# Retention and softplus FFN on one core: the first unit in whole chunks, with later weight loads and an exchanged pair of heads

## Chip, cores and metric

One core of a Trainium2 chip. The metric is the device time of the kernel in microseconds; before the change the median of three runs is 817.8 us (817.5 to 818.37).

## What is computed

```python
def _attn_ref(q, k, v):                       # batch 8, heads 8, sequence 576, head dim 64
    scores = 1.0 / np.sqrt(D_) * np.matmul(q, k.transpose(0, 1, 3, 2))
    gamma = 1.0 - 2.0 ** (-5.0 - np.arange(H))
    Dmat = np.where(rel >= 0, gamma[:, None, None] ** rel[None, :, :], 0.0)
    return np.matmul(scores * Dmat, v)

def _moe_ref(x, w_in, w_out):                 # 4608 tokens, 512 -> 2048 -> 512
    h = x @ w_in
    g = np.maximum(h, 0.0) + np.log1p(np.exp(-np.abs(h)))
    return g @ w_out
```

The result is `_moe_ref(_attn_ref(q, k, v))`, the heads side by side as the 512 model columns. `w_in` and `w_out` arrive as 64-bit floats.

## The kernel before

**Retention.** The 4608 tokens are 36 *chunks* of 128. A chunk is two *steps*: step 2c holds heads 0 to 3 of chunk c, step 2c+1 heads 4 to 7. A step has two pairs of heads (`s`), and a head of 64 rows fills half of the array's rows. Per step TensorE makes the *scores* (keys by queries, L195; in the opening L360), the *sums* (keys by values, from which a running state is made, L211; L375), the *values* product (masked scores by values, L299; L397) and the *cross* product (earlier state by queries, L311; L402). Around them: the values are scaled (`scale_values`, L188 on GpSimd, L191 on ScalarE), the scores masked (`scores_out` L253, `masked_whole` L367, VectorE), the state updated (`states_out`, L280 to L293; `state_whole`, VectorE and GpSimd), and the result x put in `xt` as a high and a low part (`halves_out`, `half_x`; `values_out`).

**FFN.** A *unit* is 512 tokens. In the first unit, the loop `for i in range(NF)` goes over the 16 blocks of 128 hidden columns: h(i) (`hidden_mm`, 12 matmuls of 128x512, L475), softplus of it (ScalarE: Abs L483, Exp L484, Ln L485; VectorE: `softplus` L489), its split in a high part (ScalarE, `softplus_split` L493) and a low one (VectorE, `softplus_rest` L497), together g(i), then y(i) (`output_mm`, 12 matmuls, L510 or L518), which is issued one iteration later, behind h(i+1). Each of the two PSUM banks of h serves every other i.

**Weights.** Each block has two *pieces* of 128x512, win (for h) and wout (for y). A piece is loaded (`load_weight` L564, 512 KB) in one of five buffers and turned into high and low parts by five operations, which the text calls p (ScalarE, `weight_p` L574), t (VectorE, L581), b (VectorE, L587), c (ScalarE, L599) and d (VectorE, L604). After d the buffer's next load is issued and a win is written back to DRAM (`weight_store` L608).

**The opening** does steps 0 to 7 (the first unit's tokens) before the loop, loads in a hand-written order on SP's queue, and also handles step 8's scores and sums and three weight pieces. In the loop every odd i does one attention step: scores and sums of step m, values and cross of step m-1, in a bank of their own. After the loop come ten *plain slots* p (product L892, retention of a whole chunk at every even p by `chunk_products`, y of the slot before), then the rest, whose code stays. `chunk_products` takes two steps at once in two banks, `two` (scores and results) and `third` (sums). Since two row groups of the array must not write one bank at once, a tiny memset on GpSimd (`mark`) stands between the sums of the first row group and those of the second.

Engines run their own instructions in the order written; a wait holds up all that is behind it. What sets the order is the code's own order.

```python
    first_a, first_b = {3: 0, 5: 1, 6: 2}, {4: 0, 6: 1}
    first_weights = {4: (0,), 6: (1,), 7: (2,), 8: (3,)}
```

Of the kernel before, what the change touches and what calls it, by code (L numbers as in the profile page):

```python
# [40 lines left out]
START_WEIGHTS = 3  # L41
OPENING = 3
NOPEN = AHEAD + 2
# [3 lines left out]
NPIECE = 2 * NF  # L47
NJ = NF // 2
OPEN1 = 6
# [20 lines left out]
LAST = 320  # L70

# [13 lines left out]
def retention_softplus_ffn(ctx: ExitStack, tc, first, whole, others, consts, w, out):  # L85
# [6 lines left out]
    const, att, moe = pool("const", 1), pool("att", 2), pool("moe", 2)  # L92
    rawp, xpool, wpool = pool("rawp", 2), pool("xpool", 1), pool("wpool", 1)
# [8 lines left out]
    later = {}  # L102
# [47 lines left out]
    def load_rest(m):  # L150
        place = later["odd"] if m >= 2 * CHUNKS - 1 and m % 2 else rawp
# [7 lines left out]
    def load_step(m):  # L159
# [8 lines left out]
        else:  # L168
            if m < NOPEN:
                place = openp if m < OPEN1 else openp2  # L170
                r = place.tile([P, 8 * C if m < FIRST else RAW], F32, name=f"raw{m}")
# [9 lines left out]
    def scale_values(m):  # L181
# [5 lines left out]
        if m >= AHEAD:  # L187
            nc.gpsimd.tensor_mul(v, v, f.unsqueeze(2).broadcast_to([P, 4, D]))  # L188
            return
# [16 lines left out]
    def sums_mm(m, s, t, h):  # L206
# [3 lines left out]
        if follows if t else start != HC:  # L210
            mm = nc.tensor.matmul(L["T"][rows[h], t, part[s]], L["kp"][rows[t], s, rows[h]], L["v"][rows[t], s, rows[h]],  # L211
                                  start=True, stop=True, skip_group_check=True)
            L.setdefault(("sums", t), []).append(mm)
# [83 lines left out]
    def values_mm(m, s, t, h, clear):  # L297
        L = live[m]
        nc.tensor.matmul(L["O"][rows[h], t, part[s]], L["v"][rows[t], s, rows[h]], L["a"][rows[t], h, s],  # L299
                         start=clear, stop=L["states"][t] is None, skip_group_check=True)  # L300

    def cross_mm(m, s, t, h):
# [4 lines left out]
        if t == h:  # L307
# [16 lines left out]
    def chunk_products(steps, done):  # L324
# [18 lines left out]
        for n in range(max(len(x) for x in pairs)):  # L343
            if n == 2 * len(steps) and sums_of(steps, 0):
                mark = nc.gpsimd.memset(later["mark"].tile([1, 1], F32, tag="mark", name="mark"), 0.0)
# [25 lines left out]
    def sums_whole(m, bank):  # L371
        L = live[m]
        for s in range(2):
            for h in range(2):
                nc.tensor.matmul(bank[rows[h], 0, TCOLS][:, part[s]], L["kp"][:, s, rows[h]], L["v"][:, s, rows[h]],  # L375
# [16 lines left out]
    def values_whole(m, bank):  # L392
        L = live[m]
        before = states.get(m % 2)
        for s in range(2):
            for h in range(2):
                nc.tensor.matmul(bank[rows[h], s, VCOLS], L["v"][:, s, rows[h]], L["a"][:, h, s], start=True,  # L397
                                 stop=before is None, skip_group_check=True)
# [81 lines left out]
    def logs(h):  # L480

        ab = moe.tile([P, T], F32, tag="ab", name="ab", bufs=ABUFS)
        nc.scalar.activation(ab, h, AF.Abs)  # L483
        nc.scalar.activation(ab, ab, AF.Exp, scale=-1.0)  # L484
        nc.scalar.activation(ab, ab, AF.Ln, bias=1.0)  # L485
        return ab

# [73 lines left out]
    def load_weight(n):  # L561
        if n < NPIECE:
            wl[n] = wst.tile([P, PIECE, 2], I32, tag="wst", name="wst", bufs=WBUFS)
            nc.sync.dma_start(wl[n].rearrange("p c a -> p (c a)"), w[n // 2, n % 2])  # L564
# [24 lines left out]
    def weight_dst(n):  # L589
        p = n // 2  # L590
        if n % 2:
# [14 lines left out]
    def weight_store(n):  # L606
        if n < NPIECE and n % 2 == 0:
            nc.sync.dma_start(split[n // 2].bitcast(F32), wins[n // 2].bitcast(F32))  # L608
# [88 lines left out]
    first_a, first_b = {3: 0, 5: 1, 6: 2}, {4: 0, 6: 1}  # L697
    first_weights = {4: (0,), 6: (1,), 7: (2,), 8: (3,)}
    fill = moe.tile([P, T], F32, tag="ab", name="fill", bufs=ABUFS)
    nc.vector.memset(fill, 1.0)  # L700
    for m in range(AHEAD):
        load_step(m)
        for n in first_weights.get(m, ()):
            load_weight(n)
    load_step(AHEAD)
    nc.sync.dma_start(consts_sb, consts)
# [13 lines left out]
    def next_scores(m):  # L720
        new = ps_open.tile([P, 2, T], F32, tag="pair", name="pair")
        if m < FIRST:
            scores_whole(m, new)
        else:
            scores(m, new)
        return new
# [4 lines left out]
    for m in range(AHEAD):  # L731
        if m < FIRST:
            bank = (ps_att if m % 2 else ps_val).tile([P, 2, T], F32, tag="bank" if m % 2 else "val", name="bank")
            sums_whole(m, bank)
            values_whole(m, bank)
            if m == 0:
                next_scores(1)
            if m + 2 < AHEAD:
                new = next_scores(m + 2)
            ready = live[m]  # L740
            if m < FIRST - 1:
                state_whole(m, ready)
            if m == 0:
                scale_values(1)
            if m + 2 < AHEAD:
                scale_values(m + 2)
            parts_out = values_out(m, nc.gpsimd if m < FIRST - 1 else nc.vector)
            if m == 0:
                masked_whole(1)
            if m + 2 < FIRST:  # L750
                masked_whole(m + 2)
            if m == FIRST - 1:
                weight_b(2)
            parts_out()
            if m == FIRST - 1:
                weight_c(2)
            if m == FIRST - 1:
                scale_values(AHEAD)
                state_whole(m, ready)
        else:  # L760
            sums(m, new)
            scores_out(m)
            states_out(m)
        if m in first_a:
            weight_a(first_a[m])
        if m in first_b:
            weight_b(first_b[m])
            weight_c(first_b[m])
        if m == 5:
            weight_dl(0)  # L770
        if m == AHEAD - 1:
            weight_d(2)
        if m == AHEAD - 2:
            load_step(AHEAD + 1)
    weight_dl(1)
    load_weight(WBUFS + 2)
    weight_store(2)
# [5 lines left out]
    constant[0] = constants(consts_sb[:, 0:SMALL], consts_sb[:, SMALL:])  # L783


    for i in range(NF):
        n = START_WEIGHTS + 2 * i
        m = AHEAD + (i - 1) // 2
        step = i % 2
        if step:  # L790
            bank = ps_att.tile([P, 2, T], F32, tag="bank", name="bank")
            scores(m, bank)
            sums(m, bank)
            values(m - 1, bank)
            if i < NF - 1 and m + 1 >= NOPEN:
                load_step(m + 1)
        weight_p(n)
        weight_t(n)
        weight_c(n - 1)
        if i == 1:  # L800
            weight_dl(n - 1)
        weight_b(n)
        if i:
            weight_t(n + 1)
        h = hidden_mm(i, i % 2)
        ab = logs(h)
        if i > 1:
            weight_dl(n - 1)
        if i < NF - 1:
            softplus(h, ab)  # L810
        if i == 0:
            weight_t(n + 1)
        if step:
            _, t, cols = place(m - 1)
            where = (B11, B21)[(m - 1) % 2], STAGE[(m - 1) % 2, t], cols
            halves_out(m - 1)
            scores_out(m)
            states_out(m)
            if i < NF - 1:
                scale_values(m + 1)  # L820
            if m == NOPEN:
                open_pools.close()
                place_weights(ctx.enter_context(tc.tile_pool(name="wpool2", bufs=1)), NF)
        if i == NF - 1:
            softplus(h, ab)
        weight_c(n)
        if not step:
            weight_dl(n)
        gs[0, i] = softplus_split(ab)
        softplus_rest(gs[0, i], ab)  # L830
        if step:
            weight_dl(n)
            half_x(*where, nc.gpsimd)
        weight_p(n + 1)
        weight_b(n + 1)
        if n + 2 >= NPIECE and "ring" not in later:
            weight_pools.close()
            for name, bufs in (("ring", RING), ("odd", 2)):
                later[name] = ctx.enter_context(tc.tile_pool(name=name + "2", bufs=bufs))
            load_step(2 * CHUNKS - 1)  # L840
            scale_values(2 * CHUNKS - 1)
# [8 lines left out]
    for name, bufs in (("quad", QUADS), ("mark", 2), ("sum", 1)):  # L850
        later[name] = ctx.enter_context(tc.tile_pool(name=name + "2", bufs=bufs, side="right"))
    two = later["two"] = ps_att.tile([P, 2, T], F32, tag="bank", name="two")
# [4 lines left out]
    groups = [([m + 1], [m])]  # L857
    for ch in range(m // 2 + 1, NCHUNK + 1):
        groups.append(([2 * ch, 2 * ch + 1] if ch < NCHUNK else [], [k for k in (2 * ch - 2, 2 * ch - 1) if k > m]))
    groups = groups[::-1]  # L860

    def next_steps(steps):
        ks = [k for m in steps for k in ((m + 1, m + 2) if len(steps) == 1 else (m + 2,)) if k < NSTEP]
# [11 lines left out]

    def values_taken(steps, done):
        if steps:
            scores_out(*steps)
        if done:
            halves_out(*done)  # L880

    def group_out(steps, done):
        values_taken(steps, done)
        if steps:
            states_out(*steps)
# [12 lines left out]
    def plain_slot(u, p, xa, xb, rest, group=None, blocks=(), jobs=(), starts=()):  # L898
# [3 lines left out]
        ahead = u == 1 and p == 0  # L902
        if ahead:
            chunk_products(*group)
            coming_steps = next_steps(group[0])
# [7 lines left out]
        if ahead:  # L913
            group_out(*group)
        elif group:
# [5 lines left out]
        if group and not ahead:  # L921
# [78 lines left out]
    def store_out(j):  # L1000
# [3 lines left out]
        (0, prepare, PLAIN + 1), (0, prepare_whole, PLAIN), (0, prepare_sums, PLAIN), (1, prepare_split, PLAIN),  # L1004
# [6 lines left out]
        *[(2 * j + 1, store_plain, j) for j in range(PLAIN)])  # L1011
# [443 lines left out]
```

## Time and profile before

| what | us |
|---|---|
| median of the runs (lowest, highest) | 817.8 (817.5, 818.37) |
| span of the profiled execution, first to last instruction | 815.8 |
| TensorE busy | 808.2 |
| VectorE busy | 560.6 |
| ScalarE busy | 389.2 |
| GpSimd busy | 123.7 |

The profiled execution's own time is given as its span; the runs' median is 2.0 us above it. TensorE's granted clock is 1.000 of full speed over the span. Where TensorE is busy, time goes only if it has less to do; where it is idle, if what it waits for comes sooner.

### The profile page before, as it was taken

How to read it: one execution, taken by the hardware profiler on the slowest of the kernel's cores; microseconds unless marked ns; L12 is line 12 of the kernel's file. 1: busy time of each engine (PE TensorE's matmuls, PEld its weight loads, DVE VectorE, ACT ScalarE, POOL GpSimd, SP SyncE). 2: the span in 40 equal slices, each digit the busy share in tenths (PEclk: the TensorE clock that was granted, in tenths of full speed). 3: DMA queues.
4: the chain of work that ended last, by engine and by line, in shares of the span. 5: the costliest groups of instructions: out<-in, count | busy, mean ns of one | idle time of the engine just before them, and what ended most of it. 6: DMA issues, size and time to landing. Idle time of an engine off the chain costs nothing.

```text
span 815.8 us, 18681 instructions
## 1 busy us (share of the span) xinstructions
PE 808.2 (99%) x7322; PEld 666.2 (82%) x7322; DVE 560.6 (69%) x953; ACT 389.2 (48%) x681; POOL 123.7 (15%) x223
## 2 busy tenths in 40 slices
PE   8999999999999999999999999999999999999998
PEld 6788888888888888888888888888888888888886
DVE  5999976777666774867669974555679944335785
ACT  6888863334323244434344554324355734434553
POOL 4322321320321420112122001112100000000000
PEclk9999999999999999999999999999999999999999
DMA  9998979989899882798987777878657776666674
GB/s 359 324 318 292 313 239 389 334 312 324 264 311 359 304 315 79 239 330 271 310 286 236 220 229 244 261 235 264 215 177 217 221 246 193 196 191 194 194 221 159
DMA packets 149847, 211.75 MB, mean 260 GB/s; under 512 B 10880, under 2 KB 114816, under 8 KB 149760
## 3 DMA queue, kind: packets, MB, share of 16 engines
q1 hardware_dynamic: 149760, 210.56, 78.3%
q8 instruction: 59, 0.97, 0.5%
q14 instruction: 28, 0.23, 0.1%
HBM read 168.05 MB, written 42.47 MB: 258 GB/s over the span
## 4 chain that ended last, share of the span: by engine, by line
PE 95%; DMA 2%; DVE 2%; ACT 0%; issue 0%; SPq 0%; DVEq 0%
PE acc L892 22%; PE sum L1183 20%; PE y L518 16%; PE two L892 14%; PE h L475 5%; PE two L1183 4%; PE third L892 3%; PE third L211 2%; PE third L1183 2%; PE acc L1183 2%; PE two L195 2%; PE two L299 2%; PE two L311 1%; DMA raw<-others 1%; DMA raw<-whole 1%; DVE wst L587 0%
## 5 line engine op out<-in xcount | busy, mean ns | idle before, releaser
L892 PE MATMUL acc<-xt,ring 128*128 128x512 f32 x780 | 196.4, 389 | 0.1
L892 PEld LDWEIGHTS acc<-xt,ring 128*128 128x128 f32 x780 | 146.3, 188 | 30.9 <-issue 0.3
L1183 PE MATMUL sum<-parts,ring 128*128 128x512 f32 x708 | 170.9, 392 | 0.0
L1183 PEld LDWEIGHTS sum<-parts,ring 128*128 128x128 f32 x708 | 131.6, 188 | 27.8
L1177 DVE TENSOR_TENSOR parts<-g,parts 128x512 fp32r<-128x512 f32 x168 | 115.4, 694 | 45.0 <-ACT parts L1173 42.3
L518 PE MATMUL y<-wout,g 128*128 128x512 f32 x564 | 137.2, 392 | 0.3 <-DVE g L497 0.3
L1173 ACT CAST parts<-g 128x512 fp32r<-128x512 f32 x168 | 103.9, 622 | 67.6 <-DVE parts L1177 27.3
L518 PEld LDWEIGHTS y<-wout,g 128*128 128x128 f32 x564 | 104.8, 188 | 22.9 <-DVE g L497 0.7
L892 PE MATMUL two<-xt,ring 128*128 128x512 f32 x486 | 123.3, 389 | 0.0
L892 PEld LDWEIGHTS two<-xt,ring 128*128 128x128 f32 x486 | 91.2, 188 | 18.9
L1205 ACT ACTIVATE g<-g 128x512 f32<-128x512 f32 x72 | 45.3, 629 | 59.4 <-DVE g L1220 35.6
L188 POOL TENSOR_TENSOR qv<-qv,consts_sb 128x256 f32<-128x256 f32 x61 | 47.4, 778 | 164.7 <-DMA qv<-others 157.7
L1220 DVE TENSOR_TENSOR g<-two,g 128x512 f32<-128x512 f32 x24 | 16.6, 692 | 77.8 <-PE two L892 77.8
L1218 ACT COPY g<-acc 128x512 f32<-128x512 f32 x24 | 14.1, 588 | 77.6 <-PE acc L892 77.6
L497 DVE TENSOR_TENSOR g<-ab,g 128x512 fp32r<-128x512 f32 x42 | 32.3, 769 | 26.4 <-ACT g L493 25.7
L493 ACT CAST g<-ab 128x512 fp32r<-128x512 f32 x42 | 26.1, 621 | 46.2 <-PE y L518 41.5
L475 PE MATMUL h<-xt,win 128*128 128x512 f32 x192 | 47.4, 396 | 0.3 <-DVE win L604 0.3
L475 PEld LDWEIGHTS h<-xt,win 128*128 128x128 f32 x192 | 35.3, 188 | 8.2 <-DVE win L604 0.6
L1258 ACT ACTIVATE g<-acc 128x512 f32<-128x512 f32 x24 | 14.3, 598 | 49.3 <-PE acc L892 49.3
L211 PEld LDWEIGHTS third<-qv,keys 64*64 64x64 f32 x776 | 27.0, 134 | 8.9 <-issue 7.7
L253 DVE TENSOR_TENSOR a<-two,mask 128x512 f32<-128x512 f32 (+1 forms) x28 | 19.0, 679 | 22.2 <-PE third L211 15.2
L1183 PE MATMUL two<-parts,ring 128*128 128x512 f32 x144 | 33.6, 389 | 0.0
(177 smaller groups left out, 1190.4 us busy)
## 6 DMA issues: line engine op xcount, KB each, us to landing
ring<-split SPq DMA_DIRECT2D x121, 256.0 KB, 4.9
ring<-combined SPq DMA_DIRECT2D x108, 256.0 KB, 3.9
ring<-outcombined SPq DMA_DIRECT2D x96, 256.0 KB, 3.5
qv<-others SPq DMA_DIRECT2D x61, 320.0 KB, 5.5
ring<-outsplit SPq DMA_DIRECT2D x72, 256.0 KB, 3.8
wst<-w SPq DMA_DIRECT2D x32, 512.0 KB, 5.8
keys<-others SPq DMA_DIRECT2D x61, 256.0 KB, 5.4
split<-win SPq DMA_DIRECT2D x16, 512.0 KB, 6.7
```

What stands on the lines that cost most here:

```text
L188: nc.gpsimd.tensor_mul(v, v, f.unsqueeze(2).broadcast_to([P, 4, D]))
L211: mm = nc.tensor.matmul(L["T"][rows[h], t, part[s]], L["kp"][rows[t], s, rows[h]], L["v"][rows[t], s, rows[h]], start=True, stop=True, ski ...
L253: nc.vector.tensor_mul(a[:, :, at], src.rearrange("p h (s c) -> p h s c", c=HC), mask.unsqueeze(1).unsqueeze(1).broadcast_to([P, 2, 2 * le ...
L475: nc.tensor.matmul(h, wins[p][:, a, kt * P:(kt + 1) * P], xt[:, b, T1 + half, kt % 2], start=(n == 0), stop=(n == 3 * NKT - 1))
L493: nc.scalar.copy(g[:, HI], ab)
L497: nc.vector.tensor_sub(g[:, LO], ab, g[:, HI].bitcast(F32))
L518: nc.tensor.matmul(ys[u][tt], g[:, a, tt * P:(tt + 1) * P], wouts[p][:, b], start=(p == 0 and n == 0), stop=(p == NF - 1 and n == 2))
L892: nc.tensor.matmul(bank, w[:, ta, kt * P:(kt + 1) * P], xt[:, tb, x, kt], start=start and k == 0, stop=k == 5, skip_group_check=True)
L1173: nc.scalar.copy(t[:, HI], g_slot(J, n))
L1177: nc.vector.tensor_sub(t[:, LO], g_slot(J, n), t[:, HI].bitcast(F32))
L1183: nc.tensor.matmul(bank[m], w[:, a, m * P:(m + 1) * P], t[:, b], start=start and n == 0, stop=n == 2, skip_group_check=True)
L1205: nc.scalar.activation(c, c, AF.Softplus)
```

## The change

1. **Exchanged pair.** The host lays out the second pair of heads (`s` = 1) of keys, queries and the state's decay with its two heads exchanged. States then stand at rows `h ^ s`. In the opening the four cross matmuls of a step run in the four 64x64 quarters of the array instead of twice in two of them.
2. **First unit in chunks.** The loop takes chunks 4 to 8 with `chunk_products` at i = 1, 4, 8, 12 and 15 (table `GROUPS`: the chunk whose scores and sums are made, and the one whose values are), instead of one step at each odd i. `third` lies in the h bank of the other parity. Step loads and scalings go by the tables `LOADS` and `SCALES`. Slot p = 0 has no retention any more.
3. **Weights.** `PIECES` sets the order win0, win1, wout0, win2, wout1, ... The opening loads step 7 before weights 1 to 3, processes piece 0, and begins 1 and 2. In iteration i: d of win(i+1), then piece 2i+2 (c, d), and t, p, b of the next two.
4. **Order.** Step 8 leaves the opening; the softplus calls of ScalarE stand between weight operations; y(15) is issued before slot 0.

SP's queue in the opening (`raw` + number is a step's load, in the changed kernel steps 7, 8 and 9 are the three unnumbered `raw` in this order; `wst` is a weight load). Before:

```order
L564 DMA wst_199<-w 128x1024
L172 DMA raw5_201<-whole 128x1024
L172 DMA raw6_203<-whole 128x1024
L564 DMA wst_205<-w 128x1024
L172 DMA raw7_207<-whole 128x1024
L564 DMA wst_209<-w 128x1024
L172 DMA raw8_211<-others 128x1152
L564 DMA wst_213<-w 128x1024
L172 DMA raw9_215<-others 128x1152
L706 DMA consts_sb_105<-consts 128x524
L564 DMA wst_218<-w 128x1024
```

and changed:

```order
L564 DMA wst_202<-w 128x1024
L180 DMA raw5_204<-whole 128x1024
L180 DMA raw6_206<-whole 128x1024
L180 DMA raw_208<-whole 128x1024
L564 DMA wst_210<-w 128x1024
L564 DMA wst_212<-w 128x1024
L564 DMA wst_214<-w 128x1024
L180 DMA raw_216<-others 128x1152
L705 DMA consts_sb_108<-consts 128x524
L180 DMA raw_219<-others 128x1152
L564 DMA wst_221<-w 128x1024
```

Step 7 has moved ahead of one weight load, step 8 behind three; the fifth weight load (wst_218, now wst_221) still has the same loads ahead of it.

TensorE from the last step of the opening to the second h. Before:

```order
L195 MATMUL pair<-raw_211 64x64 x8
L375 MATMUL bank<-raw_207 64x64 x4
L397 MATMUL bank<-a_whole,raw_207 64x128 x4
L402 MATMUL bank<-raw_207,s 64x128 x4
L211 MATMUL pair<-raw_211 64x64 x4
L475 MATMUL h<-xt,win_428 128x512 x12
L195 MATMUL bank<-raw_215 64x64 x8
L211 MATMUL bank<-raw_215 64x64 x4
L299 MATMUL bank<-a,raw_211 64x64 x8
```

and changed, to the start of the first chunk (`two` is scores, `third` sums):

```order
L383 MATMUL bank<-raw 64x64 x4
L405 MATMUL bank<-a_whole,raw 64x128 x4
L410 MATMUL bank<-raw,s 64x128 x4
L483 MATMUL h<-xt,win_463 128x512 x12
L483 MATMUL h<-xt,win_511 128x512 x12
L203 MATMUL two<-raw 64x64 x9
L219 MATMUL third<-raw 64x64
L203 MATMUL two<-raw 64x64
```

Nothing stands between the end of the opening and h(0) any more, and nothing between h(0) and h(1).

VectorE in iteration 0 of the changed loop (wst_210 is piece 1, then 212, 214 and 221 are pieces 2, 3 and 4):

```order
L604 TENSOR_TENSOR win1_511<-wst_210,win1_511 128x512
L587 SCALAR_TENSOR_TENSOR wst_212<-wst_212 128x512
L395 TENSOR_TENSOR s_488<-bank_493,s_417 128x128
L581 TENSOR_SCALAR wst_214<-wst_214 128x512
L604 TENSOR_TENSOR wout0_182<-wst_212,wout0_182 128x512
L581 TENSOR_SCALAR wst_221<-wst_221 128x512
L587 SCALAR_TENSOR_TENSOR wst_214<-wst_214 128x512
L489 SCALAR_TENSOR_TENSOR ab_554<-h_541,ab_554 128x512
L587 SCALAR_TENSOR_TENSOR wst_221<-wst_221 128x512
L497 TENSOR_TENSOR g_578<-ab_554,g_578 128x512
```

The t of piece 4 (wst_221) stands ahead of the softplus of h(0), which frees the bank that `third` of iteration 1 takes.

The diff, cut to what matters:

```diff
-START_WEIGHTS = 3
-NOPEN = AHEAD + 2
+STEPS1 = 14
+PIECES = [(0, 0)] + [x for i in range(NF - 1) for x in ((i + 1, 0), (i, 1))] + [(NF - 1, 1)]
+GROUPS = {1: (4, None), 4: (5, 4), 8: (6, 5), 12: (7, 6), 15: (8, 7)}
+LOADS = {1: (10,), 2: (11,), 4: (12, 13), 8: (14, 15), 12: (16, 17), 15: (18, 19)}
+SCALES = {3: (10, 11), 7: (12, 13), 11: (14, 15), 14: (16, 17)}
...
-                    nc.tensor.matmul(bank[rows[h], s, VCOLS], before[:, halves_of([m])][rows[h], s], L["q"][rows[h], s],
+                    nc.tensor.matmul(bank[rows[h], s, VCOLS], before[:, halves_of([m])][rows[h ^ s], s], L["q"][rows[h ^ s], s],
                                      start=False, stop=True, skip_group_check=True)
...
-    first_weights = {4: (0,), 6: (1,), 7: (2,), 8: (3,)}
+    first_weights = {4: (0,), 7: (1, 2, 3)}
...
+        h = hidden_mm(i, i % 2)
+        if group:
+            later["third"] = ps_h.tile([P, T], F32, tag=f"h{(i + 1) % 2}", name="third")
+            chunk_products(*group)
...
+        nc.scalar.activation(ab, h, AF.Abs)
+        weight_dl(near)
+        for k in LOADS.get(i, ()):
+            load_step(k)
...
+        weight_t(far)
+        weight_c(out_now)
+        weight_dl(out_now)
+        weight_t(out_next)
+        nc.scalar.activation(ab, ab, AF.Exp, scale=-1.0)
+        weight_p(far)
+        if group:
+            states_out(*group[0])
+        weight_b(far)
+        nc.scalar.activation(ab, ab, AF.Ln, bias=1.0)
+        weight_p(out_next)
+        softplus(h, ab)
+        weight_b(out_next)
         gs[0, i] = softplus_split(ab)
         softplus_rest(gs[0, i], ab)
+        weight_c(far)
+        if group:
+            values_taken(*group)
+            for m in group[1]:
+                _, t, cols = place(m)
+                half_x((B11, B21)[m % 2], STAGE[m % 2, t], cols, nc.gpsimd)
+        for k in SCALES.get(i, ()):
+            scale_values(k)
...
+    output_some(CPU)
     for p in range(2 * PLAIN):
-        group = groups.pop() if p % 2 == 0 else None
+        group = groups.pop() if p and p % 2 == 0 else None
```

with near = 2i+1, out_now = 2i+2, far = 2i+3 and out_next = 2i+4.

## Rows read from the trace of the kernel before

**Rows 1.** The page: TensorE's busy time, and the chain that ended last, by engine.

```profile
PE 808.2 (99%) x7322; PEld 666.2 (82%) x7322; DVE 560.6 (69%) x953; ACT 389.2 (48%) x681; POOL 123.7 (15%) x223
...
PE 95%; DMA 2%; DVE 2%; ACT 0%; issue 0%; SPq 0%; DVEq 0%
```

**Rows 2.** Chain of waits up to 60 us: start, length, what.

```profile
9.70 11.04 DMA raw<-others
...
39.35 0.61 DVE win L604
```

**Rows 3.** TensorE's timeline, opening: start, length, line, tiles, count [idle before].

```profile
15.09 0.65 PE L402 MATMUL bank<-raw,s 64*64 64x128 f32 x8
15.61 0.73 PE L360 MATMUL pair<-raw 64*64 64x128 f32 x16
...
20.88 0.46 PE L195 MATMUL pair<-raw 64*64 64x64 f32 x16 [0.64 <-DMA raw<-others]
...
22.90 3.01 PE L475 MATMUL h<-xt,win 128*128 128x512 f32 x12
```

**Rows 4.** TensorE's timeline, first unit: y(0), y(1), h(3), h(4), y(3), steps 12 and 13.

```profile
29.64 2.88 PE L510 MATMUL y<-wout,g 128*128 128x512 f32 x12
...
35.55 3.02 PE L518 MATMUL y<-wout,g 128*128 128x512 f32 x12 [0.28 <-DVE g L497]
...
40.00 3.04 PE L475 MATMUL h<-xt,win 128*128 128x512 f32 x12 [0.35 <-DVE win L604]
...
45.59 2.88 PE L475 MATMUL h<-xt,win 128*128 128x512 f32 x12
48.31 2.88 PE L518 MATMUL y<-wout,g 128*128 128x512 f32 x12
...
63.33 0.46 PE L195 MATMUL bank<-qv,keys 64*64 64x64 f32 x16
...
75.53 0.46 PE L195 MATMUL bank<-qv,keys 64*64 64x64 f32 x16
```

**Rows 5.** TensorE's timeline, plain slots: products of slots 0, 4 and 5.

```profile
120.11 3.03 PE L892 MATMUL acc<-xt,ring 128*128 128x512 f32 x12
...
143.80 2.88 PE L892 MATMUL acc<-xt,ring 128*128 128x512 f32 x12
...
151.50 1.75 PE L892 MATMUL third<-xt,ring 128*128 128x512 f32 x7
```

**Rows 6.** SP's timeline (pieces 4 and 5) and DMA landings, us, issues from 15 to 18.

```profile
15.49 5.93 SPq L564 DMA_DIRECT2D wst<-w  x2
...
wst<-w SPq DMA_DIRECT2D x1, 512.0 KB, 10.1
```

**Rows 7.** Timelines of ScalarE and VectorE, iteration 0.

```profile
25.95 0.60 ACT L483 ACTIVATE ab<-h 128x512 f32<-128x512 f32 x1 [0.81 <-PE h L475]
28.67 0.62 ACT L493 CAST g<-ab 128x512 fp32r<-128x512 f32 x1
...
27.95 0.68 DVE L489 SCALAR_TENSOR_TENSOR ab<-h,ab 128x512 f32<-128x512 f32 x1
28.55 0.42 DVE L581 TENSOR_SCALAR wst<-wst 128x512 int32<-128x512 uint32 x1
```

**Rows 8.** Timelines of VectorE and GpSimd, 35 to 39 us.

```profile
36.22 1.10 DVE L587 SCALAR_TENSOR_TENSOR wst<-wst 128x512 int32<-128x512 int32 x1
37.24 0.97 DVE L581 TENSOR_SCALAR wst<-wst 128x512 int32<-128x512 uint32 x1
...
35.72 1.06 POOL L188 TENSOR_TENSOR raw<-raw,consts_sb 128x256 f32<-128x256 f32 x1
36.74 1.19 POOL L444 TENSOR_TENSOR xt<-xs,xt 128x256 fp32r<-128x256 f32 x1
```

**Rows 9.** Windows: busy (count) PE, PEld, DVE, ACT, POOL; clock, DMA share, GB/s.

```profile
30.00:35.00 5.00, 5.00 (x24) 3.92 (x22) 4.41 (x11) 4.37 (x9) 0.00 (x0) 1.00 0.94 323
35.00:40.00 5.00, 4.37 (x70) 3.20 (x69) 4.90 (x8) 3.72 (x7) 3.10 (x4) 1.00 0.81 270
```

More of the change, by code (lines that the diff above doesn't have):

```diff
@@ L374, in sums_whole @@
             for h in range(2):
[L375 removed]
+                nc.tensor.matmul(bank[rows[h ^ s], 0, TCOLS][:, part[s]], L["kp"][:, s, rows[h]], L["v"][:, s, rows[h]],
                                  start=True, stop=True, skip_group_check=True)
@@ L396, in values_whole @@
             for h in range(2):
-                nc.tensor.matmul(bank[rows[h], s, VCOLS], L["v"][:, s, rows[h]], L["a"][:, h, s], start=True,
+                nc.tensor.matmul(bank[rows[h], s, VCOLS], L["v"][:, s, rows[h]], L["a"][:, h ^ s, s], start=True,
                                  stop=before is None, skip_group_check=True)
@@ L606, in weight_store @@
     def weight_store(n):
-        if n < NPIECE and n % 2 == 0:
-            nc.sync.dma_start(split[n // 2].bitcast(F32), wins[n // 2].bitcast(F32))
+        p, second = PIECES[n]
+        if not second:
+            nc.sync.dma_start(split[p].bitcast(F32), wins[p].bitcast(F32))
     def weight_dl(n):
@@ L720, in next_scores @@
     def next_scores(m):
[L721 to L726, printed above, removed]
+        scores_whole(m, ps_open.tile([P, 2, T], F32, tag="pair", name="pair"))
     next_scores(0)
@@ new lines, in retention_softplus_ffn @@
+    summed = []
+    for m in range(FIRST):
+        bank = (ps_att if m % 2 else ps_val).tile([P, 2, T], F32, tag="bank" if m % 2 else "val", name="bank")
+        sums_whole(m, bank)
+        values_whole(m, bank)
+        if m == 0:
+            next_scores(1)
+        if m + 2 < FIRST:
+            next_scores(m + 2)
+        summed.append(live[m])
+        if m < FIRST - 2:
+            state_whole(m, summed[m])
+        if m == 0:
+            scale_values(1)
+        if m + 2 < FIRST:
+            scale_values(m + 2)
+        parts_out = values_out(m, nc.gpsimd if m < FIRST - 1 else nc.vector)
+        if m == 0:
+            masked_whole(1)
+        if m + 2 < FIRST:
+            masked_whole(m + 2)
+        if m == 4:
+            weight_b(0)
+        if m == 5:
+            weight_c(0)
+        if m < FIRST - 1:
+            parts_out()
+        if m == 3:
+            weight_a(0)
@@ new lines, in retention_softplus_ffn, with values_taken, group_out, chunk_steps @@
+    place_weights(ctx.enter_context(tc.tile_pool(name="wpool2", bufs=1)), NF)
+    two = later["two"] = ps_att.tile([P, 2, T], F32, tag="bank", name="two")
+    def values_taken(steps, done):
+        if steps:
+            scores_out(*steps)
+        if done:
+            halves_out(*done)
+    def group_out(steps, done):
+        values_taken(steps, done)
+        if steps:
+            states_out(*steps)
+    def chunk_steps(ch):
+        return [] if ch is None else [2 * ch, 2 * ch + 1]
+    for i in range(NF):
+        near, out_now, far, out_next = 2 * i + 1, min(2 * i + 2, NPIECE - 1), 2 * i + 3, 2 * i + 4
+        if i == NF - 1:
+            near = NPIECE
+        elif i == NF - 2:
+            far, out_next = NPIECE, NPIECE - 1
+        group = [chunk_steps(ch) for ch in GROUPS.get(i, ())]
+        h = hidden_mm(i, i % 2)
+        if group:
+            later["third"] = ps_h.tile([P, T], F32, tag=f"h{(i + 1) % 2}", name="third")
+            chunk_products(*group)
+            if i == ODD:
+                open_pools.close()
+                later["odd"] = ctx.enter_context(tc.tile_pool(name="odd2", bufs=2))
+        ab = moe.tile([P, T], F32, tag="ab", name="ab", bufs=ABUFS)
+        nc.scalar.activation(ab, h, AF.Abs)
+        weight_dl(near)
+        for k in LOADS.get(i, ()):
+            load_step(k)
+        if not i:
+            weight_b(out_now)
+            state_whole(FIRST - 1, summed[FIRST - 1])
+            for m in (FIRST, AHEAD):
+                scale_values(m)
+        weight_t(far)
[11 more added lines that the diff above has]
+        weight_b(out_next)
@@ L837, in retention_softplus_ffn @@
+        if i >= NF - 2 and "ring" not in later:
             weight_pools.close()
[L838 to L841, printed above, removed]
+            later["ring"] = ctx.enter_context(tc.tile_pool(name="ring2", bufs=RING))
             for _ in range(RING):
@@ L920, in plain_slot @@
         gs[u, p] = softplus_split(ab)
-        if group and not ahead:
+        if group:
             values_taken(*group)
@@ L1407, in tokens, with turned @@
         return a.transpose(0, 2, 1, 3).reshape(NCHUNK, C, 2, 2, 2, D)
+    def turned(a, pair, head):
+        a = np.moveaxis(a.copy(), (pair, head), (0, 1))
+        a[1] = a[1, ::-1].copy()
+        return np.moveaxis(a, (0, 1), (pair, head))
     def crossed(a):
```

171 lines of the change are left out of this document (34 added, 137 removed).

## The prediction

> **What bounds the kernel now.** I read the page first. TensorE is busy for 808.2 of 815.8 us and holds 95% of the chain that ended last [rows 1]: only less TensorE work, or one of the 7.6 us in which it is idle, can shorten the run. The change touches the first 135 us, so I read that stretch alone. In the chain of waits a load of step 8 stands until 20.7 us, and behind it VectorE work until 39.96 us, when win3 lets h(3) go [rows 2]. So up to 40 us the bound is first the loads, then VectorE, though TensorE looks busy. TensorE's timeline shows what that costs in waits: 0.64 us for step 8 [rows 3], 0.28 us at y(1) and 0.35 us at h(3) [rows 4]. From h(4) on TensorE runs without a gap; a block of twelve 128x512 matmuls takes 48.31 - 45.59 = 2.72 us [rows 4].
>
> The sum is made against the profiled execution, which is known by its span, 815.8 us; the runs' median is 2.0 us above it, and I carry each gain over unchanged.
>
> **The change, part by part.**
>
> *Attention in chunks.* In the old loop one step comes back every 75.53 - 63.33 = 12.20 us [rows 4], of which four blocks are 10.88: a step costs 1.32 us. A whole chunk in the plain slots costs 151.50 - 143.80 - 2 x 2.72 = 2.26 us [rows 5], 0.38 less than two steps. From h(4), 45.59 us [rows 4], to the first product, 120.11 us [rows 5], the old order takes 74.52 us: 24 blocks (65.28) and 9.24 of attention. The new one has in the same stretch, with y(15) counted behind as before, 24 blocks and four chunks (i = 4, 8, 12, 15): 65.28 + 9.04 = 74.32. Slot 2 then does a whole chunk where it had one and a half; that costs between nothing and 2.26 - 1.32 = 0.94 us, I take the middle, 0.47. This part alone **loses 0.27 us**; its gain lies before h(4), where steps 8 to 11 had their turns at i = 1 and 3 and in the opening.
>
> *Opening.* Step 7 no longer waits behind weight 1, step 8 leaves with its wait of 0.64 us and its scores and sums, about 0.6 us [rows 3]. The exchanged pair lets four cross matmuls run side by side: before they take 15.61 - 15.09 = 0.52 us a step [rows 3], in six steps. The gain is between nothing and half, 1.56 us; I take the upper end, since the scores, which use all four quarters, get 16 instructions done in little more than the cross product's time for 8. So TensorE could reach h(0) some 2.8 us before its 22.90 us [rows 3], near 20.1, minus the last split of x, which keeps h(0) from ending before about 22.9. h(1) needs win1, whose d stands right there on VectorE: about 23.0 to 25.7.
>
> *Start of the loop.* Most of this lead is not kept. The sums of chunk 4 at i = 1 go in the bank of h(0), so TensorE waits for the softplus of h(0); ahead of it on VectorE stands the t of piece 4. Piece 4 is issued at 15.49 and lands 10.1 us later, at 25.6 [rows 6], and it has the same loads ahead of it as before. From there: t 0.42, b 0.68, softplus 0.68, high part of g 0.62 [rows 7], where b is priced as the softplus, which has its shape: y(0) starts at 28.0 instead of 29.64 [rows 4]. That is also why the exchanged pair is worth almost nothing by itself: without it h(1) would end near 27.0 and y(0) start by about 28.1. y(0) ends at 30.7. h(2) must wait until VectorE has read `third`, six operations behind that high part (low part, d, t, d, t, copy: about 4 x 0.62 + 2 x 0.4 = 3.2 at the same rows): 31.2, **a new wait of 0.5 us**. Then h(2), y(1), h(3), y(2) run with no attention between them, 10.88 us, and h(4) starts at 42.1 instead of 45.59. **Gain up to h(4): 3.5 us.** It holds the two old waits (0.28 and 0.35) and the turn of i = 3.
>
> *Loads.* Between piece 4 and the chunk at i = 4, step 11 must come through: eight 512 KB transfers of weights, two or three write-backs and two steps, some 6.4 MB. At the 323 GB/s of 30 to 35 us, with the engines 0.94 busy [rows 9], that is 19.9 us, to 45.5; the chunk begins at 44.8 and reads scaled values of step 11 late in its first half. I price this at 0 to 1 us and leave it in the range.
>
> *Chain of g.* Old: from Abs at 25.95 to softplus at 27.95, high part at 28.67, which takes 0.62 [rows 7], and 0.68 for the low part, 4.0 us. Now a c and a p stand between ScalarE's three calls, 2 x 0.6 more: 5.2 to 5.3 with the start. y(i) comes 2 x 2.72 = 5.44 us after h(i). That hides it by 0.15 us where no chunk stands at i or i+1: i = 2, 5, 6, 9, 10, 13. If this cover goes, TensorE waits there, and nothing later gives it back. What can break it is GpSimd. Next to GpSimd's scaling and split, b took 1.10 instead of 0.68 and t 0.97 instead of 0.42 [rows 8]: about 0.5 us for each GpSimd operation that meets VectorE. After each of the chunks at i = 4, 8 and 12 two scalings and two splits of x run in those iterations. I count one of them on the chain, 0.5 - 0.15 = 0.35, three times: **1.0 us lost**. The bounds are 0 and rival B.
>
> *End of the loop.* y(15) ahead of slot 0 needs g(15) 5.0 us after h(15) (a chunk and y(14)), about as long as its chain; 0 to 0.3 us, taken as 0. From slot 0's product to its y only the product of slot 1 lies between, 2.72 us, and softplus, high and low part take 0.6 + 0.62 + 0.68 = 1.9. Nothing.
>
> **Sum:** 3.5 - 0.27 - 1.0 = 2.2 us less: 817.8 - 2.2 = **815.6** (span 813.6).
>
> **Rivals.**
>
> *A. The exchange does not make the quarters run together.* For it: no row shows cross products in four quarters. The lead into the wait for piece 4 shrinks, y(0) comes 0.1 us later: 815.7. Chance 0.10.
>
> *B. GpSimd on the chain of g.* Both scalings after a chunk fall on it: 2 x 0.5 - 0.15 = 0.85, three times 2.55: 817.8 - 3.5 + 0.27 + 2.55 = 817.1. For it: scalings start as soon as their loads land, and these land one or two iterations after the chunk. Against: VectorE often stands idle for Ln, so part is hidden. The Trainium skill ("SBUF — State Buffer", section "Terms") says that VectorE and GpSimd share a port pair that is locked for a whole instruction, the loser being fully blocked; by it the b at 36.22 starts only when the scaling ends at 36.78, and its end at 37.32 [rows 8] agrees within 0.15 us. By that rule a scaling met at its start costs up to 1.06 us instead of 0.5. Chance 0.22.
>
> *C. The loads become the bound in iterations 0 to 4: slower.* One mechanism: the chunk at i = 4 waits for step 11's scaling. At the 270 GB/s of 35 to 40 us [rows 9], 6.4 MB take 23.7 us, to 49.3, and scaling it 1.06 [rows 8] more, to 50.4, against a chunk at 44.8: 5.6 us lost, 817.8 - 2.2 + 5.6 = 821.2. It decides from a rate below about 290 GB/s, when the loss passes 3.8 us. Against: the engines were only 0.81 busy at that rate, so it was not the limit. Chance 0.12.
>
> *D. Fewer waits than I count.* The copy of `third` and GpSimd cost nothing: 3.5 + 0.5 - 0.27 = 3.7, 814.1. Chance 0.06.
>
> **How the numbers follow.** The forecast has 0.50. What a measurement of this kernel can tell from no change is 0.2%, 1.6 us, so faster means below 816.2 and slower above 819.4. Faster: 0.43 of the forecast's 0.50 (its own range 814.2 to 816.6), 0.09 of A, 0.02 of B, all of D: 0.60. Slower: 0.02 of B and 0.12 of C: 0.14. The rest, 0.26, is the same. The range leaves out what is beyond B's upper part and D's lower: 813.6 to 818.8.
>
> **What would show it.** In the new profile: h(0) near 20 us and no load wait in the opening after step 6; cross products near 0.3 us; y(0) near 28.0 with a wait on VectorE before the first sums; a wait of half a microsecond at h(2); h(4) near 42; chunks of 2.3 us; waits of y on the low part of g only in iterations 5, 6, 9, 10 and 13. It is wrong if h(4) comes after 44 us, if GpSimd's scaling is what a chunk waits for, or if y waits for g in every iteration.

## The result and the profile after

The changed kernel takes 826.54 us (median of 4 runs, 825.51 to 826.6), the kernel before 817.97 on the same chip: ratio 1.0098, 95% interval [1.0081, 1.0116]. It is slower by 1%; forecast was 815.6, and the range (813.6 to 818.8) does not hold it. The profiled span is 823.8 us where it was 815.8, so 8.0 us longer.

The page of the changed kernel, busy times, and its group of the sums on TensorE (busy us, mean ns of one, idle before):

```profile
PE 814.8 (99%) x7322; PEld 665.0 (81%) x7322; DVE 556.0 (67%) x935; ACT 383.8 (47%) x677; POOL 117.1 (14%) x214
...
L1159 PE MATMUL sum<-parts,ring 128*128 128x512 f32 x708 | 175.1, 397 | 0.0
```

The same group of the kernel before:

```profile
L1183 PE MATMUL sum<-parts,ring 128*128 128x512 f32 x708 | 170.9, 392 | 0.0
```

TensorE has the same 7322 instructions as in [rows 1] and is busy 6.6 us longer; it is idle 1.4 us longer (9.0 us, before 7.6), and all of its new waits lie ahead of 136 us. The sums of the later units, whose code the change does not touch (L1183, now L1159), cost 4.2 us more by themselves, 6 ns on each matmul. The granted clock is 0.999 of full speed, before 1.000: a tenth of a percent, at most 0.8 us, so the clock is not the reason.

TensorE's timeline of the changed kernel, start of the loop (against [rows 4]):

```profile
28.61 0.24 PE L219 MATMUL third<-raw 64*64 64x64 f32 x1 [1.12 <-DVE ab L489]
...
29.23 3.03 PE L510 MATMUL y<-wout,g 128*128 128x512 f32 x12
32.17 3.02 PE L483 MATMUL h<-xt,win 128*128 128x512 f32 x12
...
37.77 2.91 PE L483 MATMUL h<-xt,win 128*128 128x512 f32 x12
40.52 2.91 PE L518 MATMUL y<-wout,g 128*128 128x512 f32 x12
43.27 2.91 PE L483 MATMUL h<-xt,win 128*128 128x512 f32 x12
```

Read the starts: 37.77, 40.52, 43.27. A block of twelve now takes 2.75 us, not the 2.72 of [rows 4], with no idle time in between. The plain slots of the same kernel show that this does not hold for every matmul:

```profile
121.24 2.88 PE L873 MATMUL acc<-xt,ring 128*128 128x512 f32 x12
123.96 2.88 PE L873 MATMUL third<-xt,ring 128*128 128x512 f32 x12
126.68 2.91 PE L518 MATMUL y<-wout,g 128*128 128x512 f32 x12
129.43 2.88 PE L873 MATMUL acc<-xt,ring 128*128 128x512 f32 x12
...
135.41 3.03 PE L518 MATMUL y<-wout,g 128*128 128x512 f32 x12 [1.08 <-DVE g L497]
138.28 1.98 PE L873 MATMUL third<-xt,ring 128*128 128x512 f32 x8
...
151.70 2.90 PE L873 MATMUL third<-xt,ring 128*128 128x512 f32 x12
```

The products (xt by ring) still take 123.96 - 121.24 = 2.72; y (wout by g) takes 129.43 - 126.68 = 2.75. At the product of slot 3, at 138.28, the two kernels are still level:

```profile
138.36 1.98 PE L892 MATMUL third<-xt,ring 128*128 128x512 f32 x8
```

That is the kernel before. So two things happened. Up to slot 3 a lead was won and lost again (0.08 us is left of it), and from there to the end, in code that is the same in both kernels, the run takes 823.8 - 138.28 = 685.5 us instead of 677.4: **8.1 us, all of the loss**. From the product of slot 5 on (151.70, before 151.50 [rows 5]) it is 7.8 us of them.

### The profile page after: what moved, and what is told of

The parts are those of the page before. It is cut to its first block, busy times and chain, and to the rows that moved or that the text cites. A ratio compares the mean times of both kernels' runs of the same rounds, so it can differ in the third digit from the quotient of the medians.

```text
span 823.8 us, 18643 instructions
## 1 busy us (share of the span) xinstructions
PE 814.8 (99%) x7322; PEld 665.0 (81%) x7322; DVE 556.0 (67%) x935; ACT 383.8 (47%) x677; POOL 117.1 (14%) x214
## 4 chain that ended last, share of the span: by engine, by line
PE 96%; DMA 2%; DVE 1%; SPq 1%; issue 0%; ACT 0%; DVEq 0%
PE acc L873 21%; PE sum L1159 20%; PE y L518 16%; PE two L873 13%; PE h L483 5%; PE two L1159 4%; PE third L873 3%; PE third L219 2%; PE third L1159 2%; PE acc L1159 2%; PE two L203 2%; PE two L307 2%; PE two L319 2%; DMA raw<-whole 1%; DMA quad<-split 1%; PE y L510 0%
## 5 line engine op out<-in xcount | busy, mean ns | idle before, releaser
L1159 PE MATMUL sum<-parts,ring 128*128 128x512 f32 x708 | 175.1, 397 | 0.0
L1159 PEld LDWEIGHTS sum<-parts,ring 128*128 128x128 f32 x708 | 131.6, 188 | 31.5
L518 PE MATMUL y<-wout,g 128*128 128x512 f32 x564 | 138.9, 395 | 1.1 <-DVE g L497 1.1
L196 POOL TENSOR_TENSOR qv<-qv,consts_sb 128x256 f32<-128x256 f32 x58 | 44.3, 765 | 146.9 <-DMA qv<-others 143.8
L261 DVE TENSOR_TENSOR a<-two,mask 128x512 f32<-128x512 f32 x32 | 22.0, 687 | 23.0 <-PE two L319 19.1
L1159 PE MATMUL two<-parts,ring 128*128 128x512 f32 x144 | 34.6, 395 | 0.0
```

The lines of the kernel that those rows point to most:

```text
L261: nc.vector.tensor_mul(a[:, :, at], src.rearrange("p h (s c) -> p h s c", c=HC), mask.unsqueeze(1).unsqueeze(1).broadcast_to([P, 2, 2 * le ...
L518: nc.tensor.matmul(ys[u][tt], g[:, a, tt * P:(tt + 1) * P], wouts[p][:, b], start=(p == 0 and n == 0), stop=(p == NF - 1 and n == 2))
L1159: nc.tensor.matmul(bank[m], w[:, a, m * P:(m + 1) * P], t[:, b], start=start and n == 0, stop=n == 2, skip_group_check=True)
```

## The experiments

**Theory.** The `mark` tile belongs to a pool of its own. Before, that pool was opened after the loop, behind all large tiles; the changed kernel needs it in the loop and opens it at the front:

```diff
     const, att, moe = pool("const", 1), pool("att", 2), pool("moe", 2)
+    later = {"mark": pool("mark", 2)}
     rawp, xpool, wpool = pool("rawp", 2), pool("xpool", 1), pool("wpool", 1)
...
-    for name, bufs in (("quad", QUADS), ("mark", 2), ("sum", 1)):
```

Its two buffers of 32 bytes lie in front of what is allocated behind them on that side. In the built programs the large tiles of the FFN start at these bytes of a partition, modulo 256 (the runs below show what a shift between the two rows costs, not these bytes themselves):

```
                     before   changed
xt, wout, ring          192         0
win, g, parts           192       192
```

Every product of h (xt, win), y (wout, g) and the sums (ring, parts) now has its two operands 64 apart modulo 256; the product xt by ring has not, as both moved. That is the pattern of the 2.75 and the 2.72. Rival: the new order of the work costs the time (buffers come free otherwise, transfers collide) and the longer blocks follow from it.

*pad256 and pad128* keep the changed schedule and give `mark` more buffers, 256 or 128 bytes in all instead of 64 (pad128: `4`):

```diff
-    later = {"mark": pool("mark", 2)}
+    later = {"mark": pool("mark", 8)}
```

> The changed kernel with eight mark buffers of 32 bytes per partition instead of two, so that all that is allocated behind them (xt, w_out, ring, raw) lies 256 bytes further than before the change instead of 64. Theory A (the 64 bytes of the new pool put xt, w_out and ring out of step with g, w_in and quads, and full matmuls of such pairs take 1 to 3% longer): the pitch of 128x512 matmuls is 226.7 ns again everywhere, the run comes down by 8 to 9 us, to 816 to 818 us. Theory B (the exchanged heads or the new order slow TensorE for the whole run): it stays at 825 to 827. Theory C (the granted clock of 0.999): it stays within 1 us of the changed kernel.

> The same with four mark buffers, 128 bytes instead of 64. Theory A with a grain of 128 bytes: as with 256, 816 to 818 us. Theory A with a grain of 256 bytes: still slow, 821 to 827. Theories B and C: 825 to 827.

Measured: pad256 819.07 us, 1.0005 [0.9995, 1.0015]; pad128 828.34, 1.0124 [1.0108, 1.014], a little above what was expected of a grain of 256 bytes. Six more buffers that nothing needs take the whole loss away. The time goes with the addresses, not with the schedule.

*before_shift64* makes the reverse step: the old kernel, its schedule untouched, with 64 unused bytes at that place.

```diff
+    pool("pad", 1).tile([P, 16], F32, name="pad")
```

> The kernel before with nothing changed but an unused pool of 64 bytes per partition ahead of the pools of raw data, xt and w_out. Theory A: 8 to 9 us slower than the kernel before, 826 to 827 us, with pitches of 229 ns in the first unit as in the changed kernel. Theories B and C: no change, 817.5 to 818.4.

Measured: 826.81 us, 1.0103 [1.0085, 1.0121], the loss of the changed kernel. TensorE's timeline and a group of it (lines stand one lower than in the kernel before):

```profile
47.47 2.91 PE L476 MATMUL h<-xt,win 128*128 128x512 f32 x12
50.22 2.91 PE L519 MATMUL y<-wout,g 128*128 128x512 f32 x12
```

```profile
L1184 PE MATMUL sum<-parts,ring 128*128 128x512 f32 x708 | 175.1, 397 | 0.0
```

Blocks of 2.75 us and 175.1 us of sums, as in the changed kernel, without any of its edits. That the places of the tiles are the cause is shown from both sides.

*all_even* asks whether agreement modulo 128 is enough: in the changed kernel xt, wout, ring and win are put at 128 and g and two of the four buffers of parts at 0, modulo 256.

```diff
+    pool("pad", 1).tile([P, 16], F32, name="pad")
...
-    later = {"mark": pool("mark", 2)}
+    later = {"mark": pool("mark", 4)}
...
-    edge.tile([P, 8], F32, name="edge")
+    edge.tile([P, 24], F32, name="edge")
```

> The changed kernel with all large tiles at multiples of 128 bytes: 64 bytes ahead of the left pools, 128 for mark, and the edge tile 64 bytes longer. Theory A, if what counts is that the two operands of a matmul agree: fast, 816 to 818 us. If instead an address of 64 modulo 128 is good by itself and 0 is bad: slower than the changed kernel, 830 us or more, since g, w_in and quads are now at 0 too. Theory B: 825 to 827.

Measured: 825.35 us, 1.0086 [1.0071, 1.0101]. It is not enough. TensorE's timeline in the loop, the slots and the sums:

```profile
38.04 2.92 PE L485 MATMUL h<-xt,win 128*128 128x512 f32 x12
40.80 2.96 PE L520 MATMUL y<-wout,g 128*128 128x512 f32 x12
43.59 2.91 PE L485 MATMUL h<-xt,win 128*128 128x512 f32 x12
...
122.33 2.89 PE L875 MATMUL acc<-xt,ring 128*128 128x512 f32 x12
125.05 2.89 PE L875 MATMUL third<-xt,ring 128*128 128x512 f32 x12
...
453.79 0.86 PE L1161 MATMUL acc<-parts,ring 128*128 128x512 f32 x3
454.49 0.84 PE L1161 MATMUL third<-parts,ring 128*128 128x512 f32 x3
455.17 0.84 PE L1161 MATMUL acc<-parts,ring 128*128 128x512 f32 x3
```

y, with operands 128 apart, takes 43.59 - 40.80 = 2.79; the product, whose operands agree, 2.72. In the sums, where half of the buffers of parts agree with the ring, three matmuls take 454.49 - 453.79 = 0.70 and 455.17 - 454.49 = 0.68 us by turns, as that would give; in the kernel before they take 0.68 throughout. h agrees too and takes 40.80 - 38.04 = 2.76, though; a block next to one that disagrees may lose a little as well, which is not shown.

*shift32, shift128, shift192, shift256* are before_shift64 with another number of bytes (`[P, 8]`, 32, 48, 64).

> The kernel before with one unused tile of 32 bytes per partition that moves the same tiles as the change did by half as much; no instruction is changed. Theory: what counts is the difference of the two operands' addresses modulo 256 bytes, with steps of 64 bytes; 32 bytes then cost nothing or as much as 64: 818 or 827 us. Rival: every byte of difference counts in proportion: about 822.

> The same with 128 bytes. Theory: the largest difference there is modulo 256; blocks of twelve in the first unit take 2.80 us where they took 2.72, about 828.5 us as the changed kernel with a pad of 128 took, or a little less. Rival (difference counts modulo 128): 818.

> The same with 192 bytes, which modulo 256 is 64 the other way. Theory: if the size of the difference counts and not its sign, as 64: 826.8 us, blocks of 2.75 us in the first unit. Rival (the longer the distance, the worse): above 829.

> The same with 256 bytes. Theory: addresses agree modulo 256 again, 818 us, blocks of 2.72 us. Rival (a larger grain, or the mere presence of a further pool): above 825.

Measured: 829.21 us, 1.0137 [1.0105, 1.017]; 827.9, 1.0121 [1.009, 1.0152]; 826.29, 1.0102 [1.0071, 1.0133]; 817.67, 0.9991 [0.9977, 1.0004]. One block from the start differences of each timeline, and two groups' mean of one matmul:

```
bytes   block of h or y   sum<-parts,ring   two<-xt,ring      median
  0         2.72 us            392 ns           389 ns       817.97
 32         2.80               398              389          829.21
 64         2.75               397              389          826.81
128         2.79               397              389          827.9
192         2.80               395              390          826.29
256         2.72               392              389          817.67
```

At 256 bytes all is as before, so of the sizes tried 256 bytes is the grain, and a further pool as such costs nothing. Within it the loss does not grow with the distance: a block takes 2.80 us at 32 bytes and 2.75 at 64, which refutes both "in steps of 64" and "in proportion". 192 is slower than 64 in the first unit and faster in the sums, so the sign of the difference counts as well, and not in one direction. The products, both of whose operands moved, stay within 1 ns in the column (the group acc<-xt,ring, whose blocks stand between those of y, within 3).

**The schedule alone.** With the addresses restored (pad256) the change is worth 1.0005 [0.9995, 1.0015]: nothing, where 2.2 us less were forecast. TensorE's timeline of pad256:

```profile
28.80 3.02 PE L510 MATMUL y<-wout,g 128*128 128x512 f32 x12
...
42.77 2.88 PE L483 MATMUL h<-xt,win 128*128 128x512 f32 x12
47.59 3.02 PE L518 MATMUL y<-wout,g 128*128 128x512 f32 x12
50.45 2.88 PE L483 MATMUL h<-xt,win 128*128 128x512 f32 x12
...
55.89 2.88 PE L483 MATMUL h<-xt,win 128*128 128x512 f32 x12
58.69 3.01 PE L518 MATMUL y<-wout,g 128*128 128x512 f32 x12
61.55 2.88 PE L483 MATMUL h<-xt,win 128*128 128x512 f32 x12
...
120.84 2.88 PE L873 MATMUL acc<-xt,ring 128*128 128x512 f32 x12
...
137.20 2.88 PE L873 MATMUL third<-xt,ring 128*128 128x512 f32 x12
...
146.82 0.27 PE L219 MATMUL third<-qv,keys 64*64 64x64 f32 x1 [0.91 <-POOL qv L196]
...
151.50 2.88 PE L873 MATMUL third<-xt,ring 128*128 128x512 f32 x12
```

h(4) leads by 45.59 - 42.77 = 2.82 us, slot 0's product by 120.11 - (120.84 - 2.72) = 2.0 (y(15) now stands ahead of it), slot 3's by 138.36 - 137.20 = 1.16, slot 5's by 151.50 - 151.50 = 0 [rows 4, 5]. The lead is lost in the slots. 0.5 us of it is the whole chunk that slot 2 now does (from slot 2's product at 129.00 to slot 3's, less two blocks and a wait of 0.44, are 2.32 us, before 1.79), as priced (0.47). The other 1.5 us go with two waits, those 0.44 us of a y and 0.91 us of the chunk in slot 4. Windows of the kernel before (busy and count of PE, PEld, DVE, ACT, POOL; clock, DMA share, GB/s):

```profile
0.00:110.00 110.00, 106.13 (x1098) 85.08 (x1099) 93.14 (x175) 86.13 (x170) 35.74 (x61) 1.00 0.89 317
110.00:120.00 10.00, 9.93 (x146) 7.95 (x144) 6.46 (x12) 6.50 (x12) 2.14 (x4) 1.00 0.64 198
```

and of pad256:

```profile
0.00:110.00 110.00, 105.55 (x1073) 84.25 (x1074) 89.73 (x163) 83.31 (x169) 30.75 (x54) 1.00 0.90 326
110.00:120.00 10.00, 10.00 (x148) 8.30 (x147) 5.55 (x10) 4.70 (x10) 1.31 (x4) 1.00 0.33 99
...
130.00:140.00 10.00, 9.56 (x162) 7.87 (x161) 9.12 (x19) 2.66 (x5) 1.11 (x3) 1.00 1.06 392
```

By 110 us pad256 has moved 326 GB/s x 110 us = 35.9 MB, 1.0 MB more than the kernel before (34.9). In the next 10 us it moves 99 GB/s less, so at 120 us both stand at 36.8 MB: the lead in the loads is gone. From there on the DMA engines are full in both kernels (385 GB/s in the kernel before from 130 to 140 us), and the lead is not won back: 0.99 MB are 2.5 us at 392 GB/s. Why they stand idle is on VectorE's timeline of pad256 and SP's below it, with SP's of the kernel before last:

```profile
114.54 0.69 DVE L604 TENSOR_TENSOR wout<-wst,wout 128x512 fp32r<-128x512 f32 x1 [2.82 <-ACT wout L599]
...
130.06 0.69 DVE L651 TENSOR_TENSOR quad<-quad 128x512 f32<-128x512 f32 x1 [4.32 <-DMA quad<-split]
```

```profile
115.26 5.19 SPq L637 DMA_DIRECT2D ring<-split  x8
...
123.51 1.71 SPq L646 DMA_DIRECT2D quad<-split  x2
```

```profile
114.60 5.18 SPq L636 DMA_DIRECT2D ring<-split  x8
119.87 1.02 SPq L645 DMA_DIRECT2D quad<-split  x2
```

The eight loads of the ring take the space of the weight buffers, so they go only after the d of the last piece, 31. The change puts its c (ScalarE) behind the Abs of h(15); d comes at 114.54, the ring goes at 115.26, where the kernel before issued it at 114.60. What the kernel before moves ahead of it, the last write-back of win and the load of step 17 (113.0 to 114.5 us), pad256 has long done, so its DMA engines have next to nothing to move from 110.3 us to the ring. The two quads go 3.6 us later than before: 0.7 of that is the ring, and in most of the rest the loads of steps 18 and 19 now go first (`LOADS`). So VectorE stands 4.32 us for a quad, with what y of slot 1 needs queued behind it (that y waits 0.44 us here, 1.08 in the changed kernel), and the chunk of slot 4 waits 0.91 for values that GpSimd scaled late.

*early31* takes that one thing away: pad256 with c and d of piece 31 at the end of iteration 14.

```diff
         weight_c(far)
+        if i == NF - 2:
+            weight_c(out_next)
+            weight_dl(out_next)
```

> The 256-byte kernel with c and d of the last piece (31) in iteration 14 instead of 15, so that ScalarE does c before the Abs of h(15) and the eight ring loads, which wait for that d, are issued some 2 us earlier, near 113 us. Theory D: the loads from 113 to 150 us are what the plain slots wait for, the whole stream moves 2 us ahead, the waits at slots 2 and 4 shrink, and the kernel comes out 1 to 2 us faster than the 256-byte kernel, 0.1 to 0.25% faster than before. Rival (the slots wait for GpSimd or VectorE work, not for loads): no change.

Measured: 816.45 us, 0.9978 [0.9969, 0.9987], and so better than both kernels. SP's timeline and TensorE's of it:

```profile
113.25 5.83 SPq L637 DMA_DIRECT2D ring<-split  x8
```

```profile
121.68 2.88 PE L876 MATMUL acc<-xt,ring 128*128 128x512 f32 x12
...
150.67 2.88 PE L876 MATMUL third<-xt,ring 128*128 128x512 f32 x12
```

The ring leaves 2.0 us sooner, the DMA engines move 181 GB/s from 110 to 120 us, GpSimd is waited for no more, and slot 5's product leads by 0.83 us. At slot 0 this execution led by 120.11 - (121.68 - 2.72) = 1.15, less than pad256's (it was 0.9 us later by h(14), ahead of the edit), but the slots take 0.3 us of the lead and not 2.0: slot 2's whole chunk costs what was priced, and no wait is left there.

*late_sums* moves two preparations of a later chunk from slot 0 to slot 1 in early31; *late_store* also moves the write-backs of w_out back by two slots.

```diff
-        (0, prepare_whole, PLAIN), (0, prepare_sums, PLAIN),
+        (1, prepare_whole, PLAIN), (1, prepare_sums, PLAIN),
...
-        *[(2 * j + 1, store_plain, j) for j in range(PLAIN)])
+        *[(min(2 * j + 3, 9), store_plain, j) for j in range(PLAIN)])
```

> As early31, and the two sum jobs of block 5 go from slot 0 to slot 1, behind the low part of g of slot 1 on VectorE. Theory D with VectorE held by the load of the two quads: the wait of y in slot 2 (0.44 us in the 256-byte kernel) goes, and the time falls by 0 to 0.5 us more. Rival: the wait of the chunk at slot 4 takes it back, no change to early31.

> As late_sums, and each write-back of w_out (768 KB) is issued two slots later, the last two together in slot 9. Theory D: less than before stands in the queue ahead of the loads of steps 20 and 21, the wait for their scaling at slot 4 (0.9 us in the 256-byte kernel) goes: 0.5 to 1 us faster than late_sums. Rival: the transfers are only moved behind and hold up slot 6 or 8 instead, no change.

Measured: 816.53, 0.9982 [0.9974, 0.9991]; 816.21, 0.9978 [0.9967, 0.9989]. Neither gains over early31 beyond its interval. In late_store's profile no wait of y is listed any more, so the waits of y that early31 had left were not what bounds the run.

*no_exchange* undoes the exchanged pair in pad256, in the host's layout and at the six places that index by it:

```diff
-                    nc.tensor.matmul(bank[rows[h], s, VCOLS], before[:, halves_of([m])][rows[h ^ s], s], L["q"][rows[h ^ s], s],
+                    nc.tensor.matmul(bank[rows[h], s, VCOLS], before[:, halves_of([m])][rows[h], s], L["q"][rows[h], s],
```

> The changed kernel with the mark pool of 256 bytes, and with the exchange of the second pair of heads undone (heads in their old places in keys, queries and states). Theory D (the lead of the opening is absorbed, first by VectorE's work on pieces 2 to 4 ahead of the softplus of h(0), then by the loads from 115 to 150 us): the opening's cross products take 0.52 us again, h(0) starts 1.5 us later, y(0) less than 0.6 us later, and the total stays within 0.5 us of the 256-byte kernel. Rival: what the opening loses reaches the end, plus 1.5 us.

Measured: 818.4 us, 1.0005 [0.9995, 1.0014], the same ratio as pad256. In its profile h(0) starts at 22.98 instead of 20.57 and y(0) at 31.23 instead of 28.80, so what is late in the opening was not hidden by the wait for piece 4. But this profiled execution took 820.12 us, nearly the slowest of its ten (817.45 to 820.31), and pad256's 817.68, its fastest: how much of the 2.4 us is the exchange and how much the loads of that execution stays open. In the medians the exchange is worth nothing that these runs can tell.

## Why the prediction was wrong

**The step that failed** is the first: "The change touches the first 135 us, so I read that stretch alone", and with it "I carry each gain over unchanged". The code from slot 3 on is the same, but its operands lie elsewhere, and there 8.1 us were lost (before_shift64: 826.81 without any other edit; pad256: 819.07 with all of them). No term and no rival had it. Behind it stands the sentence that where TensorE is busy, time goes only if it has less to do: here it had the same 7322 instructions and was busy 6.6 us longer. Rival C, which ended on the slower side, is not what happened: between 32.17 and the chunk of i = 4 TensorE waits nowhere for a load.

**"End of the loop: Nothing"** was wrong by 1.5 us, all that the schedule had left. I priced y(15) and the slots' softplus, but not that the move of piece 31 delays the loads of the ring. Its price: early31 against pad256 is 1.0005 - 0.9978 = 0.0027 of the time, 2.2 us (1.1 to 3.3 by the two intervals, which do not overlap), and of the 2.0 us that pad256 loses between slots 0 and 5, 1.5 are such waits. With the places and the loads of the ring put right, early31 is 0.0022 below the kernel before, 1.8 us (1.1 to 2.5), where 2.2 were forecast.

**Start of the loop**, right in kind, too large: the new wait for the softplus of h(0) is there (1.12 us, in front of `third`), and so is one at h(2), 32.17 - (29.23 + 2.75) = 0.2 at most, instead of 0.5. y(0) starts at 28.80 in pad256, not 28.0, and the gain up to h(4) is 2.82, not 3.5. What is missing lies on VectorE and GpSimd in iteration 0 of the changed kernel:

```profile
25.27 1.03 DVE L604 TENSOR_TENSOR wout<-wst,wout 128x512 fp32r<-128x512 f32 x1 [0.34 <-ACT wout L599]
26.22 0.84 DVE L581 TENSOR_SCALAR wst<-wst 128x512 int32<-128x512 uint32 x1
26.98 0.88 DVE L587 SCALAR_TENSOR_TENSOR wst<-wst 128x512 int32<-128x512 int32 x1
```

```profile
25.14 1.63 POOL L196 TENSOR_TENSOR raw<-raw,consts_sb 128x256 f32<-128x256 f32 x2
```

Three VectorE operations next to GpSimd (these two scalings and a copy of 0.47 us at 26.84) take 1.03, 0.84 and 0.88 where the same shapes take 0.69, 0.42 and 0.68 without it: 0.96 us. I had that price from [rows 8], but put it on iterations 4 to 12 and not here.

**Chain of g** held: 1.0 us was forecast over three iterations, and in pad256 y waits three times, behind the chunks of i = 4, 8 and 12, at y(5), y(9) and y(13). The timeline marks only the last as a wait (0.34 us), but the starts show all three. h(6) starts at 55.89 and y(5) at 58.69, 0.08 us late, just behind the low part of g:

```profile
57.95 0.69 DVE L497 TENSOR_TENSOR g<-ab,g 128x512 fp32r<-128x512 f32 x1
```

y(5) then takes 61.55 - 58.69 = 2.86 instead of 2.72, so this wait costs 0.22 us. y(9) at 82.91 costs 0.21 and y(13) at 107.56 costs 0.65: 1.08 in all. The last, where two scalings of GpSimd (1.81 us from 103.16 on) meet VectorE, is three times the others; that three times 0.35 came out right in sum is partly luck. **Attention in chunks** held too: the chunk of i = 4 takes 47.59 - (42.77 + 2.72) = 2.10 and 0.14 at the y behind it, 2.24 us, and the four together 9.01, where 9.04 were forecast. From h(4) to slot 0's product, y(15) left out, pad256 takes 118.12 - 42.77 = 75.35 us; 74.32 + 1.0 = 75.32 were forecast.

**Opening**: the cross product in four quarters takes half, so rival A falls. TensorE's timeline of the changed kernel (0.52 a step in [rows 3], now 12.51 - 12.24 = 0.27):

```profile
12.24 0.45 PE L410 MATMUL bank<-raw,s 64*64 64x128 f32 x8
12.51 0.62 PE L368 MATMUL pair<-raw 64*64 64x128 f32 x16
```

The wait for step 8 (0.6 us) is gone, but those for the steps before it grew from 1.1 to 1.5 us (0.64 at 8.04, 0.69 at 9.40, 0.20 at 14.52), and h(0) starts at 20.57 in pad256 and 20.99 in the changed kernel, not 20.1. Rivals B (2.55 us on the chain of g) and D (none) were both further off than the forecast's 1.0, beside a loss of 8.

## What to carry to other kernels

A small pool that moves to the front moves every tile behind it: compare the start addresses of the operands of the costliest matmuls, modulo 256 bytes, before and after an edit, and pad the difference away. When a time changes, first compare the start-to-start time of a block in code that was not edited; it tells "each is slower" from "something waits" in two rows. And when the last step of a buffer is moved, ask which loads take over its space.

## What was not expected of the hardware

A 128x512 matmul of this kernel starts every 226.7 ns when the addresses of its two operands in a partition agree modulo 256 bytes, and every 229 to 233 ns when they don't (blocks of twelve of 2.72 us against 2.75 to 2.80), at a granted clock of 0.998 to 1.000. It is the relation that counts, not a place: products xt by ring took 389 to 390 ns (two<-xt) in all six kernels of the table, wherever both operands lay. The Trainium skill ("SBUF — State Buffer", section "A bandwidth-pool intuition that's wrong (but worth ruling out)") gives TensorE a second independent read port for the load of weights. It does not speak of the operands' addresses; whoever reads from it that the places of the two can't matter to each other is put right by the runs here. What in the memory causes it was not tried. Nor is the size explained: a difference of 64 costs 2.5 ns in h and y, but 6 to 7 ns in stretches of the sums, where six matmuls of the changed kernel take 447.06 - 445.66 = 1.40 us, and 1.36 in the kernel before.
